# Moving products, pieces of a triangular inverse and logits in a delta-rule, soft-MoE and MLP kernel

## The chip, the cores and the metric

The kernel runs on one core of one Trainium2 chip. Its time is the time on the device in microseconds (us), from a launch; the median of several runs is given. A profile is one execution, taken by the hardware profiler. Its engines are PE (TensorE's matmuls), PEld (TensorE's loads of weights, beside PE), DVE (VectorE), ACT (ScalarE), POOL (GpSimd) and SP (SyncE, which issues DMAs). Each engine works through its instructions in order.

## What is computed

Three stages follow each other. The first is a delta-rule attention over 768 tokens, for 4 batches of 8 heads of width 48:

```python
for t in range(S):
    y[:, :, t] = np.einsum('bhd,bhde->bhe', q[:, :, t], state)
    v_old = np.einsum('bhde,bhd->bhe', state, kt)
    state = state + bt[:, :, :, None] * np.einsum('bhd,bhe->bhde', kt, vt - v_old)
```

Here kt is the normalised key. The result, 3072 rows of 384, goes through a soft mixture of experts (the logits are x @ phi; a softmax over the rows gives the slots, two products per expert follow, and a softmax over the slots mixes them back), and that through an MLP:

```python
d = logits - logits.max(0, keepdims=True)      # softmax over all 3072 rows
slot_input = d.T @ x
h = np.maximum(slot_input[e] @ w1[e], 0.0);  slot_out[e] = h @ w2[e]
out = c @ slot_out                             # c: softmax of logits over the slots
h = x @ w_in;  g = np.maximum(0.01 * h, h);  out = g @ w_out
```

Inputs and outputs are float32. Products that need it are made of two fp16 terms.

## The kernel before

The attention is cut into 24 steps of 32 tokens, and the 8 heads of a batch into two halves, A = 0 and 1. Within a chunk of 32 tokens the recursion is a triangular system, so each group of four steps (there are six, g) needs the inverse of a 32 x 32 unit triangle for each of 1024 (batch, head, chunk) systems. `solve(g)` makes it on VectorE, out of elementwise operations on [128, 32, 32] tiles (lines L241 to L312). It is a generator: each `yield` ends a piece, and the steps run a few pieces at a time through `bs.run(n)`. The inverse of group g + 2 begins in the last step of group g.

One step s runs like this. On PE, `ks_mm` (L406) multiplies the state by the keys for A = 0, `gram` (L200) makes products of a later step, `ks_mm` for A = 1 follows, then `qs_mm` (L417, the state by the queries, into y). ScalarE casts each half twice (L423, L424), and VectorE makes the second fp16 term (L426): these are z, called z0 for A = 0 and z1 for A = 1 below, and L426 is the last of their parts. `u_mm` (L432) multiplies the inverse by z for each half, 12 products, ScalarE copies u (L437, L440), and `s_mm` (L452) adds 24 products of keys and u to the state, whose copies st (L456) the next step's `ks_mm` reads. `mu_mm` (L463) adds the products of the chunk to y, and ScalarE copies y to xg (L825). `logits(s - 1)` transposes xg of the step before (L470), has the transpose copied to xt (L473 on ScalarE, and L476 on VectorE for a third in late steps) and multiplies it by phi (L480, three float32 matmuls; the trace counts each of them twice). Every fourth step `soft(g)` does the running softmax over rows, with L490 to L527 on ScalarE and VectorE: L513 rescales the accumulator and reads the tile mq, into which PE's L517 then writes, so that L517 waits for L513. In steps 19 and 20 and later, weights of the MLP are converted on VectorE (L560 to L603).

The order on the engines isn't that of the code: a scheduler places the instructions by priority. `behind(name)` and `tc.issue_after(ins)` tell it to issue what is within them after the latest instruction kept under that name, or after that one; `pri` shifts a priority. How many pieces of the inverse are given at each place of a step comes from four tables, by the step: `DQ` for steps up to 14 that are neither first nor last of a group and for step 0, `DQ_FIRST` for the first steps of groups, `DQ_NEXT` for the last ones, and `DQ_LAST` for steps 17 and 18, where no later inverse follows (entry [0] is read in step 0 alone):

```python
dq = DQ_NEXT if s % 4 == 3 else DQ_FIRST if s and s % 4 == 0 else DQ if s < 15 else DQ_LAST
```

Entry [1] is given out after the step's first cast, [2] after the second half's, [3] between the two halves' `u_mm`, [4] and [5] around `s_mm`, [6] ahead of the end of the step and [7] at its end. In a group's third step (s % 4 == 2) `bs.run()` gives out whatever is left.

Of the kernel before, what the change touches and what calls it, by code (L numbers as in the profile page):

```python
# [18 lines left out]
NG = 6  # L19
CHAIN_PRIO = 2000  # L20
P = dict(st=300, mu=300, x=-30, dma=-300, split=-30, wi=-100)
DQ = (8, 2, 2, 2, 2, 3, 3, 2)
DQ_LAST = (8, 5, 6, 6, 6, 8, 8, 8)
DQ_NEXT = (0, 0, 1, 1, 1, 1, 1, 0)
DQ_FIRST = (0, 5, 2, 2, 3, 3, 3, 2)
SOFT_POOL = 5
# [21 lines left out]
def drain(gen):  # L48
    for _ in gen:
        pass  # L50
# [3 lines left out]
def fused_kernel(ctx: ExitStack, tc: tile.TileContext, kq, kv, bu, phi, w1, w2, wi, wo, out):  # L54
# [103 lines left out]
    def behind(*keys):  # L158
        st = ExitStack()
        for k in keys:  # L160
            if k in end:
                st.enter_context(tc.issue_after(end[k]))
        return st
# [29 lines left out]
    def gram(s, later=None):  # L193
        k = s % 2
        c, kb = kqc[s // 2]
        gp_, tg = ((ps_g, "gm"), (ps_x, "xp"), (ps_y, "y"), (ps_m, "m"))[s % 4 if s < GALT else 0]
        gm = gp_.tile([128, 8, 64], F32, tag=tg, name="gm")
        for h in range(8):
            for bp in range(2):
                end["gm"] = pe.matmul(gm[64 * bp:64 * bp + 64, h, :], kb[:, k, bp, :, h], c[:, k, bp, :, :, h],  # L200
                                      start=(h == 0), stop=True, skip_group_check=True).ins
            if h % 4 == 3:
                yield
        if s % 4 == 0:
            gcs[s // 4] = place(AT["gc"], [128, 4, 32, 8], F32)
        with behind("nu") if s > 3 else nullcontext():
            gc_ = sc.activation(gcs[s // 4][:, s % 4].rearrange("p i h -> p h i"), gm[:, :, 0:32], AF.Copy).ins
        if s < 4:
            end["gc"] = gc_
        m = p_mm.tile([128, 2, 32, 4], F32, tag="mm", name="mm")  # L210
        mms[s] = m
        mv = m.rearrange("p a i h -> p a h i")
        gv = gm[:, :, 32:64].rearrange("p (a h) i -> p a h i", a=2)

        def mask():
            ve.tensor_tensor(mv, gv, causal.unsqueeze(1).unsqueeze(1).to_broadcast([128, 2, 4, 32]), MULT)

        if later is None:
            mask()
        else:  # L220
            later.append(mask)
        yield
# [111 lines left out]
    khs, last_s, tms = {}, [None], {}  # L334
# [20 lines left out]
    def step_k(s):  # L355
        khc = p_w.tile([128, 2, 384], F16, tag="khc", name="khc", bufs=KB)
        k1 = kvs[s // 2][:, s % 2, 0]
        sc.activation(k1, k1, AF.Copy, scale=64.0)
        kv1 = k1.rearrange("p (d a h) -> p a d h", a=2, h=4)
        k0, kl = [khc[:, l].rearrange("p (a d h) -> p a d h", a=2, h=4) for l in range(2)]  # L360
        end["k"] = sc.activation(k0, kv1, AF.Copy).ins
        after_solve(gp.tensor_tensor(kl, kv1, k0, SUB), s)
        khs[s] = khc.rearrange("p l (a x) -> p (l a) x", a=2)
# [37 lines left out]
    def ks_mm(s, A):  # L401
        kb, st = kqb[s % 2], S[A]
        for hh in range(4):
            for b in range(4):
                bp, r = b // 2, slice(32 * (b % 2), 32 * (b % 2) + 32)
                end["ks"] = pe.matmul(ksu[A][32 * b:32 * b + 32, 48 * hh:48 * hh + 48], kb[:, bp, 0, r, 4 * A + hh], st[:, bp, hh, :],  # L406
                          start=False, stop=True, skip_group_check=True).ins
# [12 lines left out]
    def z_of(s, A):  # L420
        z = p_w.tile([128, 3, 192], F16, tag=f"z{A}", name="z")
        zp = ksu[A][:, 0:192]
        sc.activation(z[:, 0], zp, AF.Copy, scale=2.0 ** -6)  # L423
        end["z"] = sc.activation(z[:, 2], zp, AF.Copy, scale=2.0 ** -17).ins  # L424
        with behind("p") if s and s % 4 == 0 and s < 20 else nullcontext():
            end["zd"] = ve.scalar_tensor_tensor(z[:, 1], zp, 2.0 ** -6, z[:, 0], MULT, SUB).ins  # L426
        return z
# [169 lines left out]
    def conv_wi(q):  # L597
        t = W[0, q] = place(3 * q, [128, 2, 768], F16)
        top = top_of(q < len(RAW), q)
        yield from from_f64(raw64.pop(("i", q)), top)  # L600
        sc.activation(t[:, 0], top, AF.Copy, scale=1024.0)
        yield
        ve.scalar_tensor_tensor(t[:, 1], top, 1024.0, t[:, 0], MULT, SUB)  # L603
        yield
# [36 lines left out]
    def load_late(s):  # L641
        with tc.issue_after(last_dma[0]):
            for x in LOADS.get(s, ()):
                if x == "w":
                    load_w()
                elif x == "i":
                    load_wi(n_wi[0])
                    n_wi[0] += 1
                else:
                    load_wo(n_wo[0])  # L650
                    n_wo[0] += 1

    def prep(s):
        step_m(s)
        step_ew(s)

    def pri(n):
        return tc.high_priority(offset=P[n]) if n in P else nullcontext()
# [16 lines left out]
    bs, bf, bc = Bg(), Bg(), Bg()  # L675
# [55 lines left out]
    with tc.issue_after(end["zd"]):  # L731
        while masks:
            masks.pop(0)()
        bs.add(solve(1))
        bs.run(DQ[0])

    for s in range(NST):
        y = ps_y.tile([128, 8, 48], F32, tag="y", name="y")
        z, u = {}, {}
        dq = DQ_NEXT if s % 4 == 3 else DQ_FIRST if s and s % 4 == 0 else DQ if s < 15 else DQ_LAST  # L740

        def ks(A):
            if s:
                ks_mm(s, A)
            z[A] = z_of(s, A) if s else first_z[A]

        with behind("mu", "lp", "x"):
            ks(0)
        with behind("z"):
            if s + 2 < NST:  # L750
                prep(s + 2)
            if s + 2 < NST - 1:
                step_k(s + 2)
        with behind("zd"):
            bs.run(dq[1])
        if s + GA < NST:
            with behind("ks"):
                drain(gram(s + GA, masks))
        with behind("gm", "k"):
            ks(1)  # L760
        with behind("zd"):
            while masks:
                masks.pop()()
        if s in (3, 7, 11, 15):
            bs.add(solve(s // 4 + 2))
        if s == 19:
            load_late(s)
        if s + 1 < NST:
            with pri("dma"):
                step_dma(s + 1)  # L770
        if s != 19:
            load_late(s)
        for x, q in CONV.get(s, ()):
            bc.add(conv_wi(q) if x == "i" else conv_wo(q))

        def conv(n=1):
            if bc.q:
                with pri("wi"), tc.issue_after(solved[NG - 1]):
                    bc.run(n)
        bs.run(dq[2])  # L780
        if s:
            with behind("ks"):
                qs_mm(s, 0, y)
                qs_mm(s, 1, y)
        lg = logits(s - 1) if s else iter(())
        with behind("y"):
            u[0] = u_mm(s, 0, z[0])
            bs.run(dq[3])
            u[1] = u_mm(s, 1, z[1])
            with behind("u"):  # L790
                next(lg, None)
            if s < NST - 1:
                for A in range(2):
                    seed(s + 1, A)
            if s > 4:
                bf.run((0, 1, 2, 9)[s % 4])
            conv()
            bs.run(dq[4])
            if s < NST - 1:
                with pri("st"):  # L800
                    s_mm(s, 0, u[0])
            conv()
            bs.run(dq[5])
            if s < NST - 1:
                with pri("st"):
                    s_mm(s, 1, u[1])
        with tc.issue_after(tms[s + (s % 4 == 3 and s + 1 < NST)]):
            if s + 4 < NST:
                load_kv(s + 4, last_u[0].ins)
        with tc.issue_after(tms[s]):  # L810
            if s + 1 < NST - 1:
                with pri("dma"):
                    step_kdma(s + 1)
            if s + 10 < NST:
                load_kq(s + 10, last_s[0])
        conv()
        bs.run(dq[6])
        with behind("y"):
            drain(lg)
            with pri("mu"), tc.issue_after(last_s[0]):  # L820
                for A in range(2):
                    mu_mm(s, A, u[A], y)
        with pri("x"):
            x = xg[s // 4 % 2][:, s % 4]
            end["x"] = sc.activation(x, y.rearrange("p h e -> p (h e)"), AF.Copy, scale=2.0 ** -12).ins  # L825
        if s % 4 == 2:
            bs.run()
        conv()
        bs.run(dq[7])
        if s and s % 4 == 0:  # L830
            bf.add(soft(s // 4 - 1))
            bf.run(1)
        free.extend(AVAIL.get(s, ()))
# [280 lines left out]
```

## Time and profile before

| | |
|---|---|
| median of 3 runs | 601.79 us (600.28 to 602.88) |
| the profiled execution | 603.62 us |
| its span, first to last instruction | 601.9 us |
| mean granted TensorE clock | 0.888 of full |
| busy share of the span | PE 85%, PEld 60%, DVE 60%, ACT 53%, POOL 34% |

The attention runs to about 321 us of the span, the weights of the MLP come in until about 376, and the MLP follows. The time before the first step (47 us) loads inputs and makes the first inverse. The shares are averages over stages that differ, so they say little of any one of them.

### The profile page before, as it was taken

How to read it: one execution, taken by the hardware profiler on the slowest of the kernel's cores; microseconds unless marked ns; L12 is line 12 of the kernel's file. 1: busy time of each engine (PE TensorE's matmuls, PEld its weight loads, DVE VectorE, ACT ScalarE, POOL GpSimd, SP SyncE). 2: the span in 40 equal slices, each digit the busy share in tenths (PEclk: the TensorE clock that was granted, in tenths of full speed). 3: DMA queues.
4: the chain of work that ended last, by engine and by line, in shares of the span. 5: the costliest groups of instructions: out<-in, count | busy, mean ns of one | idle time of the engine just before them, and what ended most of it. 6: DMA issues, size and time to landing. Idle time of an engine off the chain costs nothing.

```text
span 601.9 us, 18626 instructions
## 1 busy us (share of the span) xinstructions
PE 510.6 (85%) x7650; PEld 358.7 (60%) x7650; DVE 359.8 (60%) x1020; ACT 320.8 (53%) x783; POOL 207.1 (34%) x206
## 2 busy tenths in 40 slices
PE   7606777899998877878776978899999999999996
PEld 5505676687877775666664422566555555555553
DVE  3899786679986676989614463886333332333331
ACT  2325465567765665656542162566555555555552
POOL 9404122222313222216201000265545555555542
PEclk9765697799998797769687799999999999999999
DMA  9946567667878544896799999310101010010101
GB/s 241 249 84 155 128 155 166 160 153 159 194 160 195 120 106 96 250 265 128 201 325 418 383 410 411 108 53 1 53 0 54 2 52 1 1 54 1 53 1 52
DMA packets 70964, 87.27 MB, mean 145 GB/s; under 512 B 42720, under 2 KB 59360, under 8 KB 70880
## 3 DMA queue, kind: packets, MB, share of 16 engines
q1 hardware_dynamic: 70880, 86.09, 50.4%
q8 instruction: 60, 0.98, 0.7%
q14 instruction: 24, 0.20, 0.1%
HBM read 70.53 MB, written 4.72 MB: 125 GB/s over the span
## 4 chain that ended last, share of the span: by engine, by line
PE 60%; DVE 25%; ACT 5%; issue 4%; DMA 4%; POOL 0%; DVEq 0%; ACTq 0%; POOLq 0%
PE ops L1014 31%; DVE arena L301 4%; PE gm L200 4%; DVE arena L305 4%; DVE arena L287 3%; DMA arena<-in_w_dram 3%; PE hps L1052 3%; PE ksu L406 3%; PE xq L480 3%; PE y L463 2%; PE sps L452 2%; PE ksu L432 2%; DVE arena L274 2%; PE hn L912 1%; DVE z L426 1%
## 5 line engine op out<-in xcount | busy, mean ns | idle before, releaser
L1067 POOL TENSOR_TENSOR gl<-gf,gh 128x512 f16<-128x512 f32 x96 | 113.6, 1199 | 152.0 <-ACT gh L1066 78.3
L1014 PE MATMUL ops<-late,gh 128*128 128x384 f16 x768 | 144.1, 326 | 0.0
L1061 DVE SCALAR_TENSOR_TENSOR gf<-hps,hs 128x512 f32<-128x512 f32 x96 | 62.5, 685 | 111.0 <-ACT hs L1060 110.7
L1014 PEld LDWEIGHTS <-gh 128*128 128x128 f16 x768 | 75.1, 98 | 53.6 <-ACT gh L1066 0.3
L1060 ACT ACTIVATE hs<-hps 128x512 f32<-128x512 f32 x96 | 52.9, 594 | 56.2 <-PE hps L1052 56.1
L1014 PE MATMUL ops<-late,gl 128*128 128x384 f16 x384 | 81.7, 326 | 0.0
L1066 ACT ACTIVATE gh<-gf 128x512 f16<-128x512 f32 x96 | 60.4, 629 | 26.7 <-DVE gf L1061 20.4
L352 POOL TENSOR_TENSOR vsz<-kv,nn 128x384 f32<-128x384 f32 x24 | 23.2, 966 | 118.3 <-issue 65.6
L200 PE MATMUL gm<-kqr,arena 128*64 128x64 f32 x640 | 44.4, 312 | 17.4 <-issue 17.4
L301 DVE TENSOR_TENSOR arena<-arena 128x81 f32<-128x81 f32 (+12 forms) x150 | 54.3, 362 | 0.1
L200 PEld LDWEIGHTS gm<-kqr,arena 128*64 128x64 f32 x640 | 41.4, 222 | 19.2 <-issue 17.6
L1014 PEld LDWEIGHTS <-gl 128*128 128x128 f16 x384 | 37.6, 98 | 24.8
L305 DVE TENSOR_TENSOR arena<-arena 128x81 f32<-128x81 f32 (+12 forms) x150 | 50.5, 337 | 0.0
L287 DVE SCALAR_TENSOR_TENSOR arena<-arena 128x28 f32<-128x28 f32 (+27 forms) x186 | 47.7, 266 | 0.4
L432 PE MATMUL ksu<-z,tmb 128*128 128x48 f16 x576 | 27.2, 195 | 24.2 <-DVE z L426 24.0
L346 POOL TENSOR_TENSOR tc<-mm,tc 128x256 f16<-128x256 f32 x24 | 20.5, 854 | 64.7 <-ACT tc L345 35.8
L432 PEld LDWEIGHTS <-tmb 128*128 128x128 f16 x576 | 23.8, 118 | 28.0 <-issue 26.1
L437 ACT ACTIVATE u<-ksu 128x192 f16<-128x192 f32 x48 | 15.7, 329 | 44.9 <-PE ksu L432 42.3
L426 DVE SCALAR_TENSOR_TENSOR z<-ksu,z 128x192 f16<-128x192 f32 x48 | 16.6, 348 | 38.1 <-ACT z L424 38.0
L406 PE MATMUL ksu<-st,kqb 128*32 128x48 f32 x1472 | 35.0, 248 | 2.0 <-issue 2.0
L452 PEld LDWEIGHTS <-khb 64*128 64x128 f16 x1104 | 25.8, 115 | 17.9 <-issue 14.5
L452 PE MATMUL sps<-u,khb 64*128 64x48 f16 x1104 | 33.5, 200 | 3.3 <-issue 1.5
(176 smaller groups left out, 867.9 us busy)
## 6 DMA issues: line engine op xcount, KB each, us to landing
we<-in_w_dram SPq DMA_DIRECT2D x22, 768.0 KB, 9.8
kv<-in_kv_dram SPq DMA_DIRECT2D x24, 384.0 KB, 5.3
kqb<-in_kq_dram SPq DMA_DIRECT2D x46, 192.0 KB, 4.9
kqr<-in_kq_dram SPq DMA_DIRECT2D x20, 384.0 KB, 4.7
arena<-in_w_dram SPq DMA_DIRECT2D x10, 768.0 KB, 9.8
tmb<-tc SPq DMA_DIRECT2D x96, 64.0 KB, 3.0
arena<-in_wi_dram SPq DMA_DIRECT2D x6, 768.0 KB, 6.0
raw<-in_wo_dram SPq DMA_DIRECT2D x6, 768.0 KB, 14.9
```

Source lines behind the costliest of these rows:

```text
L200: end["gm"] = pe.matmul(gm[64 * bp:64 * bp + 64, h, :], kb[:, k, bp, :, h], c[:, k, bp, :, :, h], start=(h == 0), stop=True, skip_group_ch ...
L287: end["p"] = ve.scalar_tensor_tensor(R[:, i, 0:j], R[:, j, 0:j], gu[:, i, j:j + 1], R[:, i, 0:j], MULT, ADD).ins
L301: ve.tensor_tensor(tv, gu[:, j + 2:, j:j + 1].to_broadcast([128, n, w]), R[:, j:j + 1, 0:w].to_broadcast([128, n, w]), MULT)
L305: ve.tensor_tensor(R[:, j + 2:, 0:w], R[:, j + 2:, 0:w], tv, ADD)
L406: end["ks"] = pe.matmul(ksu[A][32 * b:32 * b + 32, 48 * hh:48 * hh + 48], kb[:, bp, 0, r, 4 * A + hh], st[:, bp, hh, :], start=False, stop ...
L432: last_u[A] = pe.matmul(ksu[A][:, 192 + 48 * hh:240 + 48 * hh], tmb[s % 2][:, a, A, :, hh], z[:, b, 48 * hh:48 * hh + 48], start=False, st ...
L452: last_s[0] = pe.matmul(sps[bp][:, A, hh, :], kb[q, a, A, :, hh], u[q, b, hh, :], start=False, stop=(s == NST - 2 and i == 2), skip_group_ ...
L1014: pe.matmul(ops[t], g[:, 128 * t:128 * t + 128], w, start=(ft == 0 and i == 0), stop=(ft == 15 and i == 2))
L1060: sc.activation(hs, hps, AF.Copy, scale=2.0 ** -12)
L1061: gf_ins = ve.scalar_tensor_tensor(gf, hps, 0.01 * 2.0 ** -12, hs, MULT, MAX).ins
L1066: sc.activation(gh, gf, AF.Copy)
L1067: gp.tensor_tensor(gl, gf, gh, SUB)
```

## The change

Four edits, none of which adds or removes an operation of the computation. In `DQ` five pieces instead of two are given out at entry [1], behind the first cast, and fewer later; the sum of entries [1] to [7] stays at 16. In `DQ_LAST` 20 pieces instead of 47 are given out in a step; what is left runs in the `bs.run()` of step 18. Entry [2]'s pieces are now behind the latest second term of z (`behind("zd")`). And the end of `logits`, its L480 products, is issued after the latest of the state's products.

```diff
--- before.py
+++ after.py
@@ -19,8 +19,8 @@
 NG = 6
 CHAIN_PRIO = 2000
 P = dict(st=300, mu=300, x=-30, dma=-300, split=-30, wi=-100)
-DQ = (8, 2, 2, 2, 2, 3, 3, 2)
-DQ_LAST = (8, 5, 6, 6, 6, 8, 8, 8)
+DQ = (8, 5, 2, 2, 2, 2, 2, 1)
+DQ_LAST = (8, 2, 3, 3, 3, 3, 3, 3)
 DQ_NEXT = (0, 0, 1, 1, 1, 1, 1, 0)
 DQ_FIRST = (0, 5, 2, 2, 3, 3, 3, 2)
 SOFT_POOL = 5
@@ -777,7 +777,8 @@
             if bc.q:
                 with pri("wi"), tc.issue_after(solved[NG - 1]):
                     bc.run(n)
-        bs.run(dq[2])
+        with behind("zd"):
+            bs.run(dq[2])
         if s:
             with behind("ks"):
                 qs_mm(s, 0, y)
@@ -815,7 +816,7 @@
                 load_kq(s + 10, last_s[0])
         conv()
         bs.run(dq[6])
-        with behind("y"):
+        with behind("y"), tc.issue_after(last_s[0]):
             drain(lg)
             with pri("mu"), tc.issue_after(last_s[0]):
                 for A in range(2):
```

What the scheduler makes of it shows in the order of instructions. On PE, near the state's products L452 of a step, this stood before:

```order
L452 MATMUL sps_155<-u,khb 128x48
L452 LDWEIGHTS khb
L452 MATMUL sps_156<-u,khb 128x48
L480 MATMUL xq<-xt,ph 32x128 x3
L452 LDWEIGHTS khb
L452 MATMUL sps_155<-u,khb 128x48
L452 LDWEIGHTS khb
```

and now, from the end of step 4 into step 5 (y, ksu, st, u and tmb as above; L406 and L417 are the next step's):

```order
L463 LDWEIGHTS tmb_71
L463 MATMUL y<-u,tmb_71 128x48
L480 MATMUL xq<-xt,ph 32x128 x3
L406 MATMUL ksu_159<-st,kqb_70 32x48 x16
L200 MATMUL gm<-kqr,arena 64x64 x16
L406 MATMUL ksu_160<-st,kqb_70 32x48 x16
L417 MATMUL y<-st,kqb_70 32x48 x32
```

L480 has moved from between the two halves of L452 to behind the L463 products, right ahead of the next step's L406; so it is in all steps but 7 and 11, where it already stood there.

On VectorE, in step 5 (ksu_159 is the half A = 0 and ksu_160 is A = 1; L287, L301 and L305 are pieces of the inverse, L216 a mask of a later step), two pieces of the difference read:

```order
 L301 TENSOR_TENSOR arena<-arena 128x216
 L287 SCALAR_TENSOR_TENSOR arena<-arena 128x12
 L305 TENSOR_TENSOR arena<-arena 128x18x12
+L426 SCALAR_TENSOR_TENSOR z<-ksu_160,z 128x192
+L216 TENSOR_TENSOR mm<-gm,causal 128x2x4x32
 L301 TENSOR_TENSOR arena<-arena 128x221
 L287 SCALAR_TENSOR_TENSOR arena<-arena 128x13
...
 L301 TENSOR_TENSOR arena<-arena 128x225
 L287 SCALAR_TENSOR_TENSOR arena<-arena 128x15
-L426 SCALAR_TENSOR_TENSOR z<-ksu_160,z 128x192
-L216 TENSOR_TENSOR mm<-gm,causal 128x2x4x32
```

The second term for A = 1 has moved ahead of eight instructions that stood before it. The like holds in steps 3, 4, 13, 14, 15 and 17.

On VectorE at the end of step 11, ahead of step 12's first L426, the order before was (the instructions from L258 to L268 are the start of the next inverse):

```order
L241 STREAM_TRANSPOSE arena<-arena 128x1024
L426 SCALAR_TENSOR_TENSOR z<-ksu_160,z 128x192
L216 TENSOR_TENSOR mm<-gm,causal 128x2x4x32
L249 TENSOR_SCALAR t_3520<-arena 128x32
L312 SCALAR_TENSOR_TENSOR tc<-tc,arena 128x3x256
L513 SCALAR_TENSOR_TENSOR acc<-acc,al,mq 128x384
L258 TENSOR_SCALAR er<-nu 128x32
L259 TENSOR_TENSOR er<-er,arena 128x32
L260 RECIPROCAL er<-er 128x32
L261 SCALAR_TENSOR_TENSOR br<-er,beta 128x32
L262 TENSOR_SCALAR arena<-br 128x32
L268 TENSOR_TENSOR arena<-arena,br 128x16x16
```

and now:

```order
L241 STREAM_TRANSPOSE arena<-arena 128x1024
L249 TENSOR_SCALAR t_3520<-arena 128x32
L312 SCALAR_TENSOR_TENSOR tc<-tc,arena 128x3x256
L258 TENSOR_SCALAR er<-nu 128x32
...
L262 TENSOR_SCALAR arena<-br 128x32
L268 TENSOR_TENSOR arena<-arena,br 128x16x16
L268 TENSOR_TENSOR arena<-arena,br 128x2x8x8
L268 TENSOR_TENSOR arena<-arena,br 128x4x4x4
L268 TENSOR_TENSOR arena<-arena,br 128x8x2x2
L268 TENSOR_TENSOR arena<-arena,br 128x16
L513 SCALAR_TENSOR_TENSOR acc<-acc,al,mq 128x384
L522 TENSOR_REDUCE cm<-lg 128x4
```

L241 has gone behind z1 (which stands above these rows now), and L513 has gone from right behind L312 to behind L268. In step 15 it stood behind L268 before too, and L241, L249 and L312, which stood ahead of z1 there, now stand behind it.

## Rows read from the trace of the kernel before

**Rows 1.** Windows by groups of steps: busy us (and instructions) by engine, clock, DMA share, GB/s.

```profile
core 0: us, PE busy (x) PEld busy (x) DVE busy (x) ACT busy (x) POOL busy (x), PEclk, DMA share, GB/s
56.50:95.40 38.90, 31.06 (x806) 26.74 (x804) 29.52 (x111) 21.64 (x64) 7.79 (x9) 0.72 0.66 156
95.40:141.10 45.70, 39.77 (x1079) 34.16 (x1078) 34.80 (x125) 29.36 (x89) 10.31 (x12) 0.85 0.62 145
141.10:182.00 40.90, 38.49 (x1083) 33.58 (x1081) 36.11 (x134) 28.41 (x90) 12.33 (x15) 1.00 0.83 178
182.00:234.20 52.20, 42.37 (x1084) 35.45 (x1081) 35.39 (x132) 29.65 (x91) 12.19 (x16) 0.81 0.56 135
234.20:293.60 59.40, 46.67 (x1029) 38.36 (x1026) 55.01 (x149) 37.13 (x110) 19.25 (x18) 0.79 0.79 207
...
321.10:376.40 55.30, 42.92 (x309) 17.43 (x308) 26.86 (x66) 19.38 (x38) 2.55 (x3) 0.91 0.99 404
```

**Rows 2.** The chain that ended last, share of the span by engine (page, section 4).

```profile
PE 60%; DVE 25%; ACT 5%; issue 4%; DMA 4%; POOL 0%; DVEq 0%; ACTq 0%; POOLq 0%
```

**Rows 3.** What PE waited for, 47 to 325 us: us in total, times, longest.

```profile
PE ksu L432 <- DVE z L426: 24.0, 13, 3.5
...
PE xq L480 <- ACT xt L473: 7.9, 15, 0.6
PE y L417 <- issue: 2.2, 1, 2.2
...
PE xq L480 <- DVE xt L476: 1.5, 2, 0.9
```

**Rows 4.** The same from 56.5, 95.4, 182.0, 234.2 us (windows of rows 1).

```profile
PE ksu L432 <- DVE z L426: 6.3, 2, 3.5
...
PE ksu L432 <- DVE z L426: 3.8, 2, 2.0
...
PE ksu L432 <- DVE z L426: 5.9, 3, 2.2
...
PE ksu L432 <- DVE z L426: 8.1, 6, 1.9
```

**Rows 5.** PE's timeline at the end of step 5: start, us, instruction, [wait].

```profile
114.94 0.55 PE L432 MATMUL ksu<-z,tmb 128*128 128x48 f16 x12 [1.78 <-DVE z L426]
...
117.65 1.49 PE L480 MATMUL xq<-xt,ph 128*32 128x128 f32 x6 [0.52 <-ACT xt L473]
...
119.66 1.15 PE L463 MATMUL y<-u,tmb 128*128 128x48 f16 x24
120.74 0.88 PE L406 MATMUL ksu<-st,kqb 128*32 128x48 f32 x32
```

**Rows 6.** PE's timeline at the end of step 9.

```profile
156.60 0.55 PE L432 MATMUL ksu<-z,tmb 128*128 128x48 f16 x12
...
158.62 0.84 PE L480 MATMUL xq<-xt,ph 128*32 128x128 f32 x6 [0.51 <-ACT xt L473]
...
159.95 0.98 PE L463 MATMUL y<-u,tmb 128*128 128x48 f16 x24
160.86 0.72 PE L406 MATMUL ksu<-st,kqb 128*32 128x48 f32 x32
```

**Rows 7.** DVE's timeline at the end of step 11.

```profile
175.67 1.23 DVE L241 STREAM_TRANSPOSE arena<-arena 128x1024 f32<-128x1024 f32 x1
...
177.59 0.94 DVE L312 SCALAR_TENSOR_TENSOR tc<-tc,arena 128x768 f16<-128x768 f16 x1
178.46 0.60 DVE L513 SCALAR_TENSOR_TENSOR acc<-acc,al,mq 128x384 f32<-128x384 f32 x1
...
180.37 0.96 DVE L268 TENSOR_TENSOR arena<-arena,br 128x256 f32<-128x256 f32 x5
```

**Rows 8.** PE's L517 in step 11.

```profile
180.07 0.33 PE L517 MATMUL mq<-ident,lt 128*128 128x128 f32 x1
```

**Rows 9.** DVE's timeline around step 9's first L426.

```profile
152.44 0.14 DVE L495 TENSOR_SCALAR nm<-mx 128x1 f32<-128x1 f32 x1
...
154.61 0.28 DVE L504 TENSOR_REDUCE sp<-pt 128x1 f32<-128x128 f32 x1
```

## The prediction, as put on record before the changed kernel ran

> **What bounds the kernel now.** I first cut the span by groups of steps and read the busy time of each engine in every cut [rows 1]. The reader should see four different regimes there. From 56.5 to 234.2 us (steps 1 to 15, in groups of three or four) TensorE is the busiest engine, but only in the group from 141.1 to 182.0 is it full: 38.49 us of 40.90, at a granted clock of 1.00. The other two groups of four steps take 45.70 and 52.20 us at 0.85 and 0.81, and the first, of three steps, 38.90 at 0.72. From 234.2 to 293.6 (steps 16 to 20) VectorE is busy 55.01 of 59.40 us. From 321.1 to 376.4 the DMA engines are at 0.99 while weights come in, and their loads are released by the attention's progress, so what the steps gain should shift this stretch along. Behind it lies the MLP, where TensorE has no such waits. The chain of work that ended last [rows 2] agrees: TensorE 60%, VectorE 25%.
>
> Then I asked what TensorE waits for in the steps [rows 3]. One wait leads: the L432 products waited 24.0 us in 13 places for the L426 second term of z on VectorE. L480, the logits' products, waited 7.9 us in 15 places for ScalarE's L473 copy, about 0.5 a step. One stall of 2.2 us stands ahead of an L417, ended by nothing the profile shows. By groups the L426 wait is [rows 4] 6.3, 3.8, 5.9 and 8.1 us, and nothing in the fast group.
>
> One slow step against one fast shows what a wait costs beyond itself. In step 5 [rows 5] the second L432 starts at 114.94 after waiting 1.78 us, and the next step's first L406 at 120.74: a tail of 5.80 us. In step 9 [rows 6] it is 156.60 to 160.86, 4.26 us, with the same instructions. Part of the difference is the clock: L480 1.49 against 0.84, L463 1.15 against 0.98, L406 0.88 against 0.72, together 0.98 us.
>
> **What each part is worth.** The mechanism on VectorE: the engine is in order and L426 for A1 (z1 below; z0 is A0's) stands behind whatever pieces of the inverse the order puts before it. By the order, the instructions between z0 and z1 go in steps 3, 4, 5, 13, 14, 15 from 4, 22, 15, 15, 16, 3 to 1, 13, 8, 9, 7, 0, in step 1 from 16 to 15, in step 17 from 6 to 5 with the piled-up work ahead falling from 41 to 27.
>
> *The z1 waits.* Step 3: 2.8 (6.3 less the longest of 3.5, which is step 1's [rows 4]); only a transpose stands ahead now, so all of it goes. Step 4, the longest of its group, 2.0: nine of 22 instructions go, and I take 1.1, about half. Step 5, 1.78 [rows 5]: half the instructions go, seven at 0.28 us (34.80/125 [rows 1]) are 2.0, I take 1.7. Steps 13 and 14, 3.7 together (5.9 less 2.2, which is step 15's): the instructions fall by six and nine, at 0.27 us (35.39/132) 1.6 and 2.4 us, so I take 3.2. Step 17: 1.0 of the 8.1 of its group. Step 1: one instruction less, 0.4 of 3.5. Sum **10.2 us**. The two ends: nothing, and all of the 16.0 us of the first three lines with a fourth of the last, 18 us.
>
> *L480 behind the state's products.* The 0.84 to 1.49 us of work stays, but L452 and L463 now run while ScalarE copies xt, so the wait of about 0.5 goes in 14 of 15 places, 7.4, and 0.7 more in a late step where VectorE makes a third of the copy. Sum **8.1 us**. What this might uncover is the state's copy st: L452 for A0 ends, and L406 of the next step needs st. Between them stood L480, L452 and L463 and now stand the same in another order, so the cover is the same; A1's st has L463 and L480 behind it, more than before. If the cover failed the 7.4 would be a wait on st instead; the lower end is 0.
>
> *The clock.* Where the waits go, the stretch is as dense as the fast group, so I expect its clock. Nine of steps 1 to 15 (1 to 5, 12 to 15) lie in groups below the full clock; I take five of their tails as recovered, 0.9 each (0.98 above): **4.5 us**, between 0 and about 9, if all nine do and L406, L200 and L417 at the step's head gain a little too.
>
> *What VectorE takes back.* The pieces do not vanish; they go behind z1. In steps 11 and 15 that has a price. L241, L249 and three quarters of L312 now stand behind z1, and L513 of the soft-MoE behind them and behind all of L258 to L268. PE's L517 waits for L513 and stands ahead of most of A1's L452, so the state waits. In step 11 of before [rows 7] L513 starts at 178.46, right behind L312, and L517 runs at 180.07 [rows 8] without a wait. Now L258 to L268 come first: from the end of L513, 179.06, to that of L268, 181.33, that is 2.27 us; L513 would end at about 181.4 and L517 would wait 1.3. ScalarE's L250 and L251, which wait for L249, also stand ahead of its L437 for A0 now, which the order puts up to 1.2 us (an L241) later. I take 2.4 us for step 11, between 0 and 3.5. In step 15 L513 already stood behind L268; L241 and L312 before it now come after z1 (1.2 and 0.9 [rows 7]), and ahead of z0 stand nine more pieces, 2.4 us, of which I take 1.6 as showing; z1's wait of 2.2 there goes: 2.1 + 1.6 − 2.2, 1.5 lost. In step 9, L495 moved behind z0, while L504, which needs its result by way of ScalarE, still stands ahead of z1. Before, 2.17 us lay between their starts [rows 9], of which ScalarE needs its part; less work lies between them now, in a step that had no wait on z. I take 1.6, between 0 and 2.2. Steps 7 and 8: 0.3. Sum **−5.8 us**, between −1 and −10.
>
> *Steps 18 to 20.* DQ_LAST changes where the last inverse's pieces stand: 27 instead of 41 behind z1 of step 17, 32 instead of 10 behind that of step 18. VectorE has 59.40 − 55.01 = 4.4 us free in the whole stretch [rows 1], so order alone can gain at most that there and I count **0** beyond step 17's 1.0 and xt. Here a rule speaks against the change. The Trainium skill ("Perfetto Trace Analysis", "Identifying the Most-Contended Engine") calls occupancy a fair measure for VectorE and says that the engine with the highest one is to be optimized first; the 93% here agrees. Were it to rule every group it would leave only VectorE's free time and not the waits; but VectorE is busy 29.52 of 38.90 and 35.39 of 52.20 us in the slow groups [rows 1], so there the rows side with TensorE's waits.
>
> *The L417 stall*, 2.2 us in one place: nothing in the change removes it, but the streams of all engines shift; half of it, **1.1**.
>
> Sum: 10.2 + 8.1 + 4.5 − 5.8 + 0 + 1.1 = 18.1 us, against the profiled execution of 603.62 us (span 601.90) 585.5. The median shown is 601.79, 1.8 lower; I predict from the median: 601.8 − 18.1 = **584 us**, 3% faster. About 0.5%, 3 us, is what a measurement of this kernel tells from no change.
>
> **Rivals.**
> *It gains more.* L513 comes in time (its inputs are there earlier too), step 9 costs nothing, and the clock stays at the fast group's level. Then −5.8 becomes −1 and 4.5 becomes 8: 26.4 us, **575**; with the stall gone and all of the first three groups' z waits too, 568 to 570. For it: the fast group, with the same work, takes 40.9 us for four steps where its neighbours take 45.7 and 52.2.
>
> *VectorE takes it back.* Its work is unchanged, and in the fast group it is busy 36.11 of 40.90 us already, so pieces behind z1 make the next z0 late. Half of the 10.2 returns and the clock gives 1: 5.1 + 8.1 + 1 − 5.8 + 1.1 = 9.5 us, **592**. Against it: the slow groups leave VectorE 9.4, 10.9 and 16.8 us free [rows 1].
>
> *It doesn't do what it says.* L480's wait is replaced by one on st, and z1's by z0's: 10.2 and 8.1 go, and −5.8 + 4.5 + 1.1 about cancel: 600 to 603.
>
> *Slower.* One mechanism: the last inverse's end. Its final transpose L308 now comes after 22 more instructions behind z1 of step 18. ScalarE's L316 waits for it, and it stands ahead of st for A1; L312 waits for L316, and all conversions of weights, then the weights' loads at share 0.99, start behind. At 55.01/149 = 0.37 us an instruction 22 are 8.1 us; that is hidden as long as step 17's 14 fewer (5.2 us) make z of step 18 early. To decide the sign it must cost over 21 us in a stretch of 59.4: then **607** or more. The profile says 3 to 8 at most.
>
> **Chances.** 584 (576 to 591 around it): 0.55. More, 575: 0.20. Taken back, 592: 0.15. No change: 0.05. Slower: 0.05. The range reaches from 569, which takes in most of the second case, to 597, with the third whole. Faster by over 0.5%: 0.90; within: 0.05; slower: 0.05.
>
> **What would show it.** The L426 wait of L432 down from 24.0 to about 12, gone in steps 3 and 14; L480 with no wait on L473; PEclk near 1.00 from 95 to 141 (0.85 now) and above 0.85 in steps 13 to 15; a new wait of L517 on L513 in steps 11 and 15, of 1 to 3 us; steps 16 to 20 at 56 to 60 us with VectorE over 90% busy; the weights at the same rate, some 18 us earlier. The prediction is wrong if z0 of steps 9, 15 and 19 comes late by as much as z1 gained, if L406 waits for st, or if the weights' stretch gets longer by what the steps gain.

## The result, and the profile after

The changed kernel takes 606.21 us (median of 8 runs, 603.17 to 608.11) against 601.84 us (8 runs, 599.54 to 603.99) before: a ratio of 1.0071, with a 95% interval of 1.0044 to 1.0099. It is slower by 0.7%, where 3% faster was forecast. Its profiled execution took 606.53 us, with a span of 604.8 us at a mean clock of 0.886.

The windows of the changed kernel by the same groups of steps, columns as in [rows 1]:

```profile
56.80:93.40 36.60, 29.74 (x800) 26.56 (x798) 28.51 (x104) 21.41 (x65) 7.74 (x9) 0.77 0.60 141
93.40:138.20 44.80, 39.59 (x1083) 35.28 (x1082) 35.16 (x125) 28.49 (x87) 10.13 (x12) 0.92 0.67 164
138.20:185.40 47.20, 39.81 (x1083) 35.09 (x1081) 39.66 (x141) 30.24 (x94) 12.64 (x16) 0.90 0.76 183
185.40:233.90 48.50, 40.95 (x1079) 35.95 (x1078) 37.44 (x131) 30.09 (x91) 11.75 (x14) 0.85 0.51 122
233.90:296.30 62.40, 48.93 (x1028) 41.04 (x1026) 54.85 (x146) 37.33 (x109) 19.34 (x18) 0.72 0.73 197
...
325.00:380.50 55.50, 43.31 (x311) 17.51 (x309) 27.72 (x67) 19.78 (x40) 2.54 (x3) 0.91 0.99 401
```

The slow groups did get shorter, by 2.3, 0.9 and 3.7 us. But the group that had been full, steps 8 to 11, takes 47.20 us where it took 40.90, its clock has fallen from 1.00 to 0.90, and steps 16 to 20 take 3.0 us more. So something new costs time where no wait on z stood before. The weights' stretch is as long as it was and merely begins later.

The waits of PE from 47 to 325 us, as in [rows 3]:

```profile
PE sps L452 <- ACT st L456: 20.6, 19, 1.3
...
PE ksu L432 <- DVE z L426: 8.9, 10, 3.1
PE mq L517 <- DVE acc L513: 4.5, 3, 1.6
PE ksu L439 <- ACT u L437: 2.9, 5, 0.9
...
PE ksu L406 <- ACT st L456: 1.2, 1, 1.2
```

The wait on z fell further than forecast, from 24.0 to 8.9 us, and L480's wait on xt is gone. In their place stands a wait that [rows 3] doesn't show: the state's products L452 waited 20.6 us, in 19 places, for L456, ScalarE's copy of the state (0.8 us, in one place, before). In each of the 19 it is the first product of A1 that waits. Step 9 shows where. This is PE's timeline of the changed kernel from its second L432 on (before: [rows 6]):

```profile
156.21 0.55 PE L432 MATMUL ksu<-z,tmb 128*128 128x48 f16 x12 [0.27 <-DVE z L426]
...
157.40 0.32 PE L452 MATMUL sps<-u,khb 64*128 64x48 f16 x8
158.85 0.82 PE L452 MATMUL sps<-u,khb 64*128 64x48 f16 x24 [1.14 <-ACT st L456]
159.61 1.15 PE L463 MATMUL y<-u,tmb 128*128 128x48 f16 x24
160.69 1.28 PE L480 MATMUL xq<-xt,ph 128*32 128x128 f32 x5
161.55 0.39 PE L406 MATMUL ksu<-st,kqb 128*32 128x48 f32 x6
```

and this ScalarE's over the same time:

```profile
157.03 0.77 ACT L440 ACTIVATE u<-ksu 128x192 f16<-128x192 f32 x2
157.69 0.48 ACT L473 ACTIVATE xt<-xq 128x384 f32<-128x384 f32 x1
158.06 0.50 ACT L399 ACTIVATE ksu<-vsz 128x384 f32<-128x384 f32 x1
158.47 0.56 ACT L456 ACTIVATE st<-sps 128x192 f32<-128x192 f32 x2
```

The last of A0's L452 is done at 157.7. ScalarE then copies xt and writes a seed (L399), and only then copies st of A0 out of `sps`, which is two tiles, with one copy for each. A0 and A1 are halves of both tiles, so A1's L452 write into the tiles that the copies read. The first copy ends at 158.80 and the second at 159.03; A1's L452 start at 158.85, right behind the first. In the kernel before, ScalarE's queue had the same order in step 9, and PE's L452 of A0 and A1 stood on either side of L480:

```profile
158.08 0.48 ACT L473 ACTIVATE xt<-xq 128x384 f32<-128x384 f32 x1
158.45 0.50 ACT L399 ACTIVATE ksu<-vsz 128x384 f32<-128x384 f32 x1
158.86 0.55 ACT L456 ACTIVATE st<-sps 128x192 f32<-128x192 f32 x2
```

```profile
157.79 0.31 PE L452 MATMUL sps<-u,khb 64*128 64x48 f16 x8
...
159.39 0.63 PE L452 MATMUL sps<-u,khb 64*128 64x48 f16 x24
```

L480's 0.84 us and the 0.51 it waited for xt made 1.35 us [rows 6], in which ScalarE copied xt, seeded and copied st. The first copy of st ended at 159.19 and A1's L452 started at 159.39, so L480 cost at most 0.2 us there. Behind L463 it keeps the next L406 back by 0.86 us (160.69 to 161.55), and the gap stays: the tail from L432 to L406 is 161.55 − 156.21 = 5.34 us, against 4.26 in [rows 6]. Some of the difference is the clock, as L463's 1.15 us against 0.98 shows.

### The profile page after: what moved, and what is told of

Read it like the earlier page. It is cut to its first block, busy times and chain, and to the rows that moved or that the text cites. A ratio compares the mean times of both kernels' runs of the same rounds, so it can differ in the third digit from the quotient of the medians.

```text
span 604.8 us, 18636 instructions
## 1 busy us (share of the span) xinstructions
PE 513.0 (85%) x7650; PEld 365.9 (60%) x7650; DVE 364.1 (60%) x1020; ACT 322.2 (53%) x783; POOL 206.0 (34%) x206
## 4 chain that ended last, share of the span: by engine, by line
PE 63%; DVE 19%; ACT 8%; DMA 6%; issue 3%; SPq 0%; DVEq 0%; POOL 0%; ACTq 0%; POOLq 0%
PE ops L1015 31%; PE gm L200 4%; DMA arena<-in_w_dram 4%; PE hps L1053 3%; PE sps L452 3%; PE y L463 3%; PE xq L480 3%; PE ksu L406 3%; PE ksu L432 2%; DVE arena L301 2%; DVE arena L305 2%; DVE arena L287 2%; DMA kv<-in_kv_dram 2%; DVE arena L274 1%; ACT ksu L399 1%
## 5 line engine op out<-in xcount | busy, mean ns | idle before, releaser
L352 POOL TENSOR_TENSOR vsz<-kv,nn 128x384 f32<-128x384 f32 x24 | 23.7, 988 | 101.9 <-issue 60.1
L301 DVE TENSOR_TENSOR arena<-arena 128x81 f32<-128x81 f32 (+12 forms) x150 | 57.4, 383 | 0.1
L452 PE MATMUL sps<-u,khb 64*128 64x48 f16 x1104 | 35.1, 197 | 25.5 <-ACT st L456 20.6
L305 DVE TENSOR_TENSOR arena<-arena 128x81 f32<-128x81 f32 (+12 forms) x150 | 53.2, 355 | 0.0
L452 PEld LDWEIGHTS <-khb 64*128 64x128 f16 x1104 | 26.8, 115 | 38.2 <-issue 32.2
L406 PE MATMUL ksu<-st,kqb 128*32 128x48 f32 x1472 | 47.8, 258 | 2.5 <-issue 1.3
L346 POOL TENSOR_TENSOR tc<-mm,tc 128x256 f16<-128x256 f32 x24 | 19.4, 807 | 82.7 <-ACT tc L345 59.4
L287 DVE SCALAR_TENSOR_TENSOR arena<-arena 128x28 f32<-128x28 f32 (+27 forms) x186 | 47.0, 263 | 0.4
L406 PEld LDWEIGHTS ksu<-st,kqb 128*32 128x32 f32 x1472 | 39.6, 156 | 5.1 <-issue 1.4
L426 DVE SCALAR_TENSOR_TENSOR z<-ksu,z 128x192 f16<-128x192 f32 x48 | 16.8, 351 | 35.1 <-ACT z L424 35.0
L432 PE MATMUL ksu<-z,tmb 128*128 128x48 f16 x576 | 26.8, 195 | 9.2 <-DVE z L426 8.9
L432 PEld LDWEIGHTS <-tmb 128*128 128x128 f16 x576 | 23.8, 118 | 13.6 <-issue 10.8
```

What stands on the lines that cost most here:

```text
L287: end["p"] = ve.scalar_tensor_tensor(R[:, i, 0:j], R[:, j, 0:j], gu[:, i, j:j + 1], R[:, i, 0:j], MULT, ADD).ins
L301: ve.tensor_tensor(tv, gu[:, j + 2:, j:j + 1].to_broadcast([128, n, w]), R[:, j:j + 1, 0:w].to_broadcast([128, n, w]), MULT)
L305: ve.tensor_tensor(R[:, j + 2:, 0:w], R[:, j + 2:, 0:w], tv, ADD)
L432: last_u[A] = pe.matmul(ksu[A][:, 192 + 48 * hh:240 + 48 * hh], tmb[s % 2][:, a, A, :, hh], z[:, b, 48 * hh:48 * hh + 48], start=False, st ...
L452: last_s[0] = pe.matmul(sps[bp][:, A, hh, :], kb[q, a, A, :, hh], u[q, b, hh, :], start=False, stop=(s == NST - 2 and i == 2), skip_group_ ...
```

## Experiments

The reading so far is called theory C (cover) below: the cost lies in the logits' move, which took the cover off ScalarE's copy of st. Its rival, theory V, is the one of the prediction that has VectorE take back what the tables gain.

**Each edit alone.** The logits' move alone, on the kernel before:

```diff
-        with behind("y"):
+        with behind("y"), tc.issue_after(last_s[0]):
             drain(lg)
```

> The kernel before with the logits' products behind the state's alone (tables and masks as before). Theory C (cover): L480 between the two halves of L452 covered the time in which ScalarE copies st of the first half, and L452 of the second half has to wait for that copy, since both halves lie in one PSUM tile. Without L480 there, L452 waits for L456 some 1.15 us a step, about 20 us in all, L480's wait on xt (7.9 us) goes, the wait of L432 on z stays near 24 us; about 0.65 us a step worse, 612 us (608 to 617). Theory V (VectorE's tables cost it): the move itself gains the xt wait, 594 us, at most 602.

Measured: 609.12 us, ratio 1.0112 (1.0062 to 1.0162). And the tables and entry [2] without that move, the line above put back in the changed kernel:

> The changed kernel with the logits' products where they were before, between the halves of the state's products: both tables and the pieces behind the second cast stay. Theory C: L432's wait on z is near 9 us as in the changed kernel (24 before), L452 hardly waits for st (about 1 us), L480 waits about 8 us for xt; 590 us (586 to 595). Theory V: the pieces behind z1 are what costs, 604 to 608 us.

Measured: 588.57 us, ratio 0.9776 (0.9721 to 0.9831). PE's waits of the first of these kernels:

```profile
PE sps L452 <- ACT st L456: 21.9, 20, 1.3
...
PE ksu L432 <- DVE z L426: 15.3, 10, 3.5
PE mq L517 <- DVE acc L513: 3.2, 3, 2.6
```

and of the second:

```profile
PE ksu L432 <- DVE z L426: 9.6, 10, 3.1
PE xq L480 <- ACT xt L473: 8.1, 16, 0.6
...
PE sps L452 <- ACT st L456: 0.8, 1, 0.8
```

Theory V falls: the tables gain 2.2% where the logits stay. The wait on st comes with the logits' move alone and goes with it. It was less bad by itself than expected (612), and the wait on z fell to 15.3 us at the same time, with the tables of before. Two things may have had a hand in that. In step 4 the same 22 instructions stand between z0 and z1 as before and the wait of 2.0 us is gone, which fits a VectorE that catches up while the steps are held by the other wait. In steps 3 and 14 the scheduler put fewer there by itself (1 for 4, 8 for 16).

**The two tables apart.** `DQ` and entry [2] alone, then `DQ_LAST` alone, each on the kernel before:

```diff
-DQ = (8, 2, 2, 2, 2, 3, 3, 2)
+DQ = (8, 5, 2, 2, 2, 2, 2, 1)
...
-        bs.run(dq[2])
+        with behind("zd"):
+            bs.run(dq[2])
```

> The kernel before with the new DQ and entry [2] behind the second cast, and nothing else: DQ_LAST and the logits' products as before. If the gain of 13 us of the kernel with all of the tables lies in steps 1 to 15, as the prediction's sum had it: L432's wait on z from 24 to about 13 us with some 8 of them in steps 16 to 20, 591 us (588 to 595). If DQ_LAST brings most of it: 597 to 602 us.

Measured: 589.54 us, ratio 0.9798 (0.9768 to 0.9827), the wait on z 14.2 us. The gain is here, in steps 1 to 15.

```diff
-DQ_LAST = (8, 5, 6, 6, 6, 8, 8, 8)
+DQ_LAST = (8, 2, 3, 3, 3, 3, 3, 3)
```

> The kernel before with the new DQ_LAST alone. The prediction counted 0 to 2 us for it, VectorE being the bound there: 600 us (597 to 603), with steps 16 to 20 at 58 to 60 us and the wait on z merely moved from step 18 to 19. If the last inverse's later end is a loss, as the rival of the prediction had it: 604 us or more. If the table carries the gain: 595 us or less.

Measured: 599.90 us, ratio 0.9977 (0.9952 to 1.0003): nothing that can be told from no change, as forecast.

**The copy of st made later, and earlier.** If L452's wait is what costs, its length should set the time. First the changed kernel with the copies of st behind the seeds of both halves:

```diff
-        for bp in range(2):
-            sc.activation(st[:, bp], sps[bp][:, A], AF.Copy)
+        with behind("seed"):
+            for bp in range(2):
+                sc.activation(st[:, bp], sps[bp][:, A], AF.Copy)
```

> The changed kernel with the suspected wait made longer: the copies of st stand behind the seeds L399 of both halves on ScalarE (one stands ahead of them now), 0.4 to 0.5 us later. Nothing else is added. Theory C: L452's wait on st (L457 here) grows from 20.6 to about 30 us, 615 us (611 to 620). If st's place on ScalarE does not set the time: 604 to 608 us.

Measured: 618.73 us, ratio 1.0284 (1.0247 to 1.0320). Of the 12.5 us over the changed kernel, 8.5 are the wait on st and 3.5 that on z. Of the kernels that move st's copy this one leaves VectorE's order nearest to the changed kernel's: the number of instructions between z0 and z1 differs by more than two only in steps 8 and 9 (13 and 9, for 7 and 12).

```profile
PE sps L452 <- ACT st L457: 29.1, 20, 1.6
...
PE ksu L432 <- DVE z L426: 12.4, 13, 2.6
```

Then the other way: `logits` gets one more yield between its transposes and the copy of xt, and that copy and the seeds go behind st.

```diff
...
-            if s < NST - 1:
-                for A in range(2):
-                    seed(s + 1, A)
...
                     s_mm(s, 0, u[0])
+            with behind("st"):
+                next(lg, None)
+                if s < NST - 1:
+                    for A in range(2):
+                        seed(s + 1, A)
```

> The changed kernel with ScalarE's copy of xt (now L474) and the seeds L399 behind the copies of st of the first half, ahead of which they stood. Theory C: st comes about 0.8 us earlier, L452's wait on L456 falls from 20.6 to 5 to 10 us, and L480 does not wait for xt, since L452 and L463 still run ahead of it; 595 us (590 to 600). Theory V: no change from the changed kernel, 604 to 608 us.

Measured: 580.45 us, ratio 0.9652 (0.9606 to 0.9698), 26 us less than the changed kernel. The waits, and the same place of step 9 on PE:

```profile
PE sps L452 <- ACT st L456: 9.6, 23, 0.5
...
PE ksu L432 <- DVE z L426: 5.6, 5, 3.1
```

```profile
151.02 0.78 PE L452 MATMUL sps<-u,khb 64*128 64x48 f16 x24 [0.41 <-ACT st L456]
151.73 0.98 PE L463 MATMUL y<-u,tmb 128*128 128x48 f16 x24
```

The wait fell from 1.14 to 0.41 us in step 9, and L481 (L480 with the line added above it) waits for ScalarE's xt nowhere: it is what the prediction hoped for, once st no longer stands behind xt. The direction and the wait are as expected; the time is 10 us below the range of that theory's number. The rest goes with the clock and with the wait on z, which fell from 8.9 to 5.6 us: from z0 of step 1 to that of step 16 the windows read, for before, the changed kernel and this one,

```profile
61.01:235.82 174.81, 148.81 (x3976) 127.19 (x3969) 131.97 (x483) 106.83 (x328) 40.69 (x48) 0.85 0.66 151
```

```profile
61.35:236.32 174.97, 147.96 (x3961) 130.80 (x3955) 136.88 (x484) 107.68 (x328) 40.80 (x49) 0.87 0.63 151
```

```profile
61.02:216.72 155.70, 140.09 (x3943) 125.37 (x3944) 133.39 (x481) 103.53 (x327) 40.23 (x48) 0.97 0.72 169
```

so that of the 19.3 us between the last two, 7.9 are PE's busy time, as its clock goes from 0.87 to 0.97, and 11.4 its idle time. The edit moved VectorE's order too (6 instructions between z0 and z1 of step 4 instead of 13, but 14 instead of 7 in step 8), so the 26 us are not the price of st's wait alone.

**Another cover.** The changed kernel with half of the L463 products in the gap:

```diff
                     s_mm(s, 0, u[0])
+            with pri("mu"), tc.issue_after(last_s[0]):
+                mu_mm(s, 0, u[0], y)
...
-                with pri("st"):
+                with pri("st"), tc.issue_after(end["mu"]):
                     s_mm(s, 1, u[1])
...
-                for A in range(2):
-                    mu_mm(s, A, u[A], y)
+                mu_mm(s, 1, u[1], y)
```

> The changed kernel with the first half of the L463 products (12 of 24, some 0.5 us) between the two halves of L452. Theory C: they cover part of the copy of st, so that L452's wait on L456 falls from 20.6 to about 10 us; 596 us (592 to 600). Theory V: no change from the changed kernel, 604 to 608 us.

Measured: 586.06 us, ratio 0.9760 (0.9704 to 0.9817); the wait on st is 10.2 us in 17 places, as expected, and the time again below the range given, by 6 us. The wait on z is lower too, 7.8 us, and so is PE's busy time: of the 21.1 us between this kernel and the changed one from z0 of step 1 to that of step 23, 13.4 are idle time and 7.7 busy time, at a clock of 0.95 against 0.87 in steps 1 to 15.

**What is left without the tables.** The seeds alone behind st, on the kernel before, with the logits where they were; then the whole cure with the tables of before.

> The kernel before, with the logits' products between the state's halves as they were and both tables, and the seeds L399 behind st. Theory C: with L480 there as the cover, L452 never waited for st, so st being 0.4 us earlier gives nothing in itself; the order on VectorE has fewer instructions between z0 and z1 in steps 4, 5, 13 and 14 (22, 15, 15, 16 before; 8, 12, 10, 8 now), so the wait of L432 on z falls from 24 to 14 to 18 us: 595 us (590 to 600). If st's place gains with L480 there as well: 585 us or less.

Measured: 587.66 us, ratio 0.9763 (0.9721 to 0.9806), the wait on z 8.7 us. That is 2 us below the range: the wait on z fell further than the order let expect (14 to 18), and st coming earlier is not told apart from it here.

> The kernel before with the logits' products behind the state's and the copy of xt and the seeds behind st, and both tables and entry [2] as before. Theory C: the move of the logits pays once st is early, whatever the tables: wait of L452 on L456 about 10 us, none on xt, L432's wait on z 15 to 24; if the two gains add, 13 us above the kernel with both: 593 us (589 to 598). If they need each other: 599 us or more.

Measured: 574.08 us (573.87 to 581.44), ratio 0.9572 (0.9511 to 0.9633), the fastest median of all and 15 us below the range that was given; its interval overlaps those of the kernel with st first and of the two below. The rows are from its execution of 581.44 us. L452's wait on st is 9.8 us and that of L432 on z 5.4 us, with the tables of before:

```profile
PE sps L452 <- ACT st L456: 9.8, 23, 0.7
PE ksu L432 <- DVE z L426: 5.4, 5, 3.1
```

So the move of the logits, with the copy of xt behind st as well, pays once ScalarE copies st first: 588 to 574 us. And the tables are not needed then: the scheduler, given other code around them, put fewer pieces between z0 and z1 by itself (in steps 4, 5 and 13 the trace has 6, 9 and 8 instructions there, against 22, 15 and 15 before).

**Both cures at once**, with the new tables and with the old:

> The changed kernel with both cures at once: the copy of xt and the seeds behind st, and half of the L463 products between the halves of L452. Theory C: the rest of the wait of L452 on L456 (9.6 us with st first alone) is shorter in each step (0.42 us) than the L463 products that now cover it (about 0.5 us), so it falls to 0 to 2 us: 573 us (570 to 577). If VectorE or the clock hold the steps by now: 579 to 582 us, as with st first alone.

Measured: 578.63 us (573.16 to 581.10), ratio 0.9605 (0.9549 to 0.9662).

> The kernel before with the logits' products behind the state's, xt and the seeds behind st, and half of the L463 products between the halves of L452; tables as before. Theory C: L452's wait on st 0 to 2 us, against 9.8 without the L463 products: 570 us (566 to 575). If the named waits no longer set the steps: 574 to 580 us, as without.

Measured: 579.07 us (577.04 to 582.12), ratio 0.9631 (0.9599 to 0.9664). Both missed what theory C expected and came out near the other number, that of waits which no longer set the steps. Neither lists a wait of L452 on st any more, but no gain can be told in the medians. The second kernel's profile shows 4.5 us ahead of L417 and as much ahead of L406 that nothing in the profile ends, in 8 places, where the kernel without the L463 products there had 4.0 and 3.0 us in 7:

```profile
PE ksu L432 <- DVE z L426: 7.4, 5, 3.1
PE y L417 <- issue: 4.5, 5, 2.2
PE ksu L406 <- issue: 4.5, 3, 2.1
```

Between the profiled executions of these two (582.12 and 581.44 us), PE's idle time from z0 of step 1 to that of step 23 fell from 27.9 to 23.7 us, and its busy time rose from 202.0 to 207.4, at a clock of 0.94 against 0.96 in steps 1 to 15. So in these two the covered wait came back as slower products. Over all executions the clocks of the two kernels overlap (0.914 to 0.933 and 0.917 to 0.932), so whether that is the rule isn't shown.

## Why the prediction was wrong

*The step that failed* is the one on L480: "Between them stood L480, L452 and L463 and now stand the same in another order, so the cover is the same". It asked who reads st, and found L406. It did not ask what has to wait for the copy itself, and that is A1's L452, which writes into the tiles that L456 reads. The term of +8.1 us had a lower end of 0. It measured 8.6 us of waits on xt saved (7.9 on L473 and 0.7 of the 1.5 on L476 [rows 3]; the other 0.9 is still there, past 325 us) and 19.8 us of a new wait on st (20.6, less the 0.8 of before), a loss of some 11 us. The kernel with that edit alone loses 7, with the wait on z down by 8.7.

The profile before had the clue. A wait of 0.5 us with 0.84 us of work behind it, between two products that seemed free to follow each other, was read as a loss of 0.5 a step; that the work fills a gap which another engine's queue leaves would have been seen on ScalarE: xt, seed and st stand in a row there, as in the rows of step 9 above. The Trainium skill ("PSUM — Partial Sum Buffer", section "PSUM bank collisions raise a hardware error") says that two engines must not access the same bank in the same partitions at once, whether they touch the same bytes or disjoint columns. By that rule the copy of one half and the products of the other must be kept apart while both lie in one bank, and the rows agree: A1's L452 waited for L456 in 19 places. What the rows show is the wait that the program sets; what an overlap would do, no run here shows. Giving each half tiles of its own was not tried.

*The z1 waits* were right in kind and nearly in size. In the steps that the term counted (1, 3, 4, 5, 13, 14 and 17) 11.4 us went, against 10.2. In all it is 15.1: 5.6 more went in steps 15, 16, 18 and 20, and 1.8 came in steps 8, 9, 11 and 12. Not all of it is the tables' doing, since the logits' move alone took 8.7 us off this wait. The kernel with the logits in place shows what the tables are worth by themselves: 588.6 us, 13.2 faster, where the prediction's terms without L480 make 10.0. The new DQ with entry [2] bring nearly all of it.

*The clock* was expected to give 4.5 us back, from nine steps below the full clock (it is eleven, 6 and 7 too); it is 0.886 against 0.888 over the span. One wait took the place of another: from z0 of step 1 to that of step 16 PE is idle for 27.0 us, against 26.0 before. Where waits went without a new one, a higher clock came: 0.95 in steps 1 to 15 of the kernel with the tables alone, 0.85 before.

*What VectorE takes back*: 5.8 forecast. L517 waits 4.5 us for L513 (0.6 before); in step 11, where 1.3 was worked out, the rows of the changed kernel are

```profile
182.34 0.60 DVE L513 SCALAR_TENSOR_TENSOR acc<-acc,al,mq 128x384 f32<-128x384 f32 x1
```

```profile
183.00 0.33 PE L517 MATMUL mq<-ident,lt 128*128 128x128 f32 x1 [1.61 <-DVE acc L513]
```

L439's wait on u grew too (2.9 us against 0.6, of which 0.7 in step 0 was there before, put down to a DMA). Steps 11 and 15 came out as worked out: in step 11 L517 and L439 take 2.3 us, against 2.4; in step 15 2.5 us, less 1.3 of the z1 wait there, against 1.5. Step 9 lost 0.3 instead of 1.6, step 8 0.8, and 1.0 came in step 19, where nothing was forecast. That is 5.6 us, with the z1 waits of steps 8, 9 and 15 that the 15.1 above has in it too: the sum held, but of its parts only the two largest.

*Steps 18 to 20* were put at nothing for `DQ_LAST`, which its own run bears out. That steps 16 to 20 take 62.4 us instead of 59.4 is only in part the new wait. In these steps and the next, 5.3 us of it took the place of 5.0 on z and 2.3 on xt that went, and of the 3.0 us only 0.7 are PE's idle time; 2.3 are its busy time, at a clock of 0.72 against 0.79. Why the clock is lower there is open.

In sum, by these waits: 15.1 + 8.6 + 0.8 (less of the stall ahead of L417) saved, 19.8 + 1.2 (L406 on st) + 3.9 + 1.6 + 1.9 (L452 on u) lost, 3.9 us to the bad. Smaller waits, 3 us in all, went besides, so the sum is rough. From z0 of step 1 to that of step 23 the changed kernel takes 4.4 us more, 2.4 of PE's idle time (41.0 to 43.4) and 2.0 of its busy time (210.6 to 212.6); the span grew by 2.9. None of the rivals was this one. The nearest, "L480's wait is replaced by one on st", had L406 waiting for st as its sign, priced the wait at what it replaced, 8 us and not 20, and had 0.05.

*What stays open*: why a rest of 0.4 us a step, once covered, gives nothing back that can be told; whether the new tables cost a little when st comes first (580 against 574 us, but the intervals overlap); and how the 26 us between the changed kernel and the one with st first divide between L452's wait (11 us), VectorE's order, which the same edit moved, and the clock.

## What to carry to other kernels

Before work is moved out of a gap, ask why there is a gap: which engine's queue will still be busy when the next instruction of the moved one comes, and what that instruction shares with it, the tile that it writes as well as the data that it reads. Work that stands between two halves of an accumulation in one PSUM tile covers the copy of the first half, and a wait inside it is not yet a loss. And a scheduler's order hangs on the whole program: an edit elsewhere can do to the wait that a table was tuned for what the table does, so gains of two edits on one wait need not add.

## What was not expected

The two gains did not add: the tables brought 13 us with the logits in the middle and 3 us with them behind (609.1 to 606.2, whose intervals overlap). Moving two short ScalarE instructions a step, the seeds, behind two others gave 2.4% by itself, with L432's wait on z down from 24.0 to 8.7 us. And the granted clock went with the length of the steps: in steps 1 to 15 it stood at 0.80 in the kernel with the longest wait (186.7 us for the 15 steps), at 0.84 to 0.87 in the four of 175 to 179 us, the kernels before and changed among them, and at 0.93 to 0.97 in those of 149 to 164. A lower clock makes the products longer in its turn, so this doesn't say which of the two sets the other.
